# Decode attention over a cached 268 MB of keys and values: units of eight heads with 64 KB value runs, in place of units of four heads with 32 KB tiles

## The chip, the cores and the metric

The kernel runs on one core of one Trainium2 chip. The metric is the device time of one execution in microseconds (us), the median over runs. Every time below comes from those runs, from the profile of one execution, or from that execution's trace.

## What is computed

Four sequences (B = 4) of one token each, model width D = 640, 32 query heads and 32 key/value heads of 128, a cache of 4096 positions, all in bfloat16. The input is normalized, and attention and a small gated MLP both start from it:

```python
xn = _layernorm(x)
# A: attention with a cache
q = (xn @ wq).reshape(B, 1, 32, 128)                     # per head
scores = einsum('bhqd,bhkd->bhqk', q, k_cache) * 128 ** -0.5
p = softmax(scores)                                      # over 4096 positions
attn = einsum('bhqk,bhkd->bhqd', p, v_cache).reshape(B, 1, 4096) @ wo
# B: gated MLP (spatial size 1)
z = gelu(xn @ w_in); z1, z2 = z[..., :864], layernorm(z[..., 864:])
mlp = (z1 * (w_sp * z2 + b_sp)) @ w_out
out = x + attn + mlp
```

The two caches hold 4 x 32 x 4096 x 128 x 2 bytes each, 134 MB. Each byte of them is needed once.

## The kernel before

**Units.** A unit is one sequence and four neighbouring heads (HT = 4), and there are NT = 32 of them, sequence fastest: unit i has sequence i % 4 and head group i // 4. The four heads' keys, 16384 rows of 128 numbers, lie in one stretch of HBM. They are cut over the 128 partitions so that partition p holds rows 128 p to 128 p + 127: 32 partitions ("lanes") for each head, one contiguous run of 32 KB for each partition. Values are laid out in the same way. A key tile or a value tile is thus 128 x 32 KB, 4 MB, one DMA on the SP queue.

**Places.** One pool of `KV_SLOTS = 5` places of 32 KB per partition serves keys and values in turn (`load`, L115); at the start three of the places hold the query weight (in two DMAs) and the MLP's weights. `pump` (L137) issues the next loads of a written list for as long as the occupant of the place, five loads earlier, has been used. The list is k0, k1, v0, k2, v1, k3 and so on, with two extra keys near the end (`EXTRA_K`), so that the last loads are values. The SP queue takes its instructions in the order written, each waiting for the readers of its place. Eight semaphores go round among the DMAs, so that a DMA also waits until the one eight before it has landed. The last value tile is loaded in four pieces (`V_CUTS`), and behind it the output weight of the last head group in four (`load_wo`, L147); the other groups' output weights are loaded one group at a time.

**One iteration (L568).** The order on PE, DVE, ACT and SP is written out by hand. For key tile i, each half of 64 rows per partition in turn:
- `product` (L399): DVE multiplies the half in place by the query, which `stage_q` (L379) has spread over the lanes two units earlier (one matmul that copies a row of queries to all partitions, then four ACT copies, one for each head's lanes).
- `fold_half` (L409): DVE adds the upper 64 numbers of each row to the lower.
- `sums` (L418): eight PE matmuls with the identity add up 64 columns to 8 in PSUM.
- `row_sums` (L429): DVE adds those 8 to the score.

Then `head_max` (L436) finds each head's maximum by a reduction, a transpose among 32 partitions and another reduction, and `exps` (L445) makes the exponentials, one ACT instruction for each head with its sum. They are written into `p_m`, a matrix of 32 columns for each group of four row positions (two sequences x four positions x four heads, zero where a head doesn't live on the partition), with which `weighted` (L462) multiplies a value tile: 32 matmul groups of 128 x 512. `weighted` for tile i runs in the iteration after its keys (later near the end). `take`, `group_den`, `group_pick`, `group_turn` and `group_proj` bring a finished head group of four sequences into the right shape, divide it by the sums and multiply it by the output weight into one PSUM tile that lives through the whole kernel.

**The ends.** Before the loop stand the normalization, the query projection (`q_rows`) and `gmlp`. After the loop, the last value tile is used position by position (`o_last`, L625) as its pieces land, then the last group's projection (L530), two copies and two output DMAs follow.

Of the kernel before, what the change touches and what calls it, by code (L numbers as in the profile page):

```python
# [12 lines left out]
ALU = mybir.AluOpType  # L13
AX = mybir.AxisListType

KV_SLOTS = 5
EXTRA_K = (24, 28)
WO_BUFS = 2
# [3 lines left out]
def kernel(  # L22
# [26 lines left out]
    HT = 4  # L49
    HG = H // HT  # L50
    NT = HG * Bsz
    LN = P // HT
    NC = HT * S // P
    HC = NC // 2
    HD2 = Dh // 2
# [6 lines left out]
    QD = 32  # L62
    CB = 4
    NG = NC // CB
    GW = CB * Dh
    MC = CB * HT

    const = ctx.enter_context(tc.tile_pool(name="const", bufs=1))
    kv = ctx.enter_context(tc.tile_pool(name="kv", bufs=KV_SLOTS))
    wop = ctx.enter_context(tc.tile_pool(name="wop", bufs=WO_BUFS))  # L70
# [5 lines left out]
    ps_m = ctx.enter_context(tc.tile_pool(name="ps_m", bufs=3, space=PSUM))  # L76
    ps_out = ctx.enter_context(tc.tile_pool(name="ps_out", bufs=1, space=PSUM))

    def slot(name):
        return kv.tile([P, SLOT], BF16, tag="kv", name=name)  # L80
# [4 lines left out]
    wq_v = A_wq.rearrange("(p c) n -> p c n", c=DC)  # L85
    wq_parts = []
    for c0, c1 in ((0, HT), (HT, DC)):
        t = slot("wq")[:, 0 : (c1 - c0) * HD].rearrange("p (c n) -> p c n", n=HD)
        nc.sync.dma_start(out=t, in_=wq_v[:, c0:c1, :])
        wq_parts += [(t, i) for i in range(c1 - c0)]  # L90
# [6 lines left out]
    w_sb = slot("w_sb")  # L97
    w_in_sb = w_sb[:, 0 : DC * F].rearrange("p (c n) -> p c n", c=DC)
    w_out_sb = w_sb[:, DC * F : DC * F + NFC * D].rearrange("p (k n) -> p k n", k=NFC)
# [6 lines left out]
    def kv_view(cache, i):  # L106
        hg, b = divmod(i, Bsz)
        return cache[b, HT * hg : HT * (hg + 1)].rearrange("h s d -> (h s) d").rearrange(
            "(p c) d -> p (c d)", c=NC
        )  # L110
# [4 lines left out]
    def load(which, i):  # L115
        cache, tiles = (A_k_cache, k_tiles) if which == "k" else (A_v_cache, v_tiles)
        t = slot("k_nat" if which == "k" else "v_nat")
        cuts = V_CUTS if (which, i) == ("v", NT - 1) else (0, NC)
        for c0, c1 in zip(cuts, cuts[1:]):
            nc.sync.dma_start(  # L120
                out=t[:, c0 * Dh : c1 * Dh], in_=kv_view(cache, i)[:, c0 * Dh : c1 * Dh]
            )
        tiles[i] = t[:].rearrange("p (c d) -> p c d", d=Dh)

    loads = [("k", 0), ("k", 1)]
    n_k = 2
    for i in range(NT):
        loads.append(("v", i))
        for _ in range(2 if i + 1 in EXTRA_K else 1):
            if n_k < NT:  # L130
                loads.append(("k", n_k))
                n_k += 1
    occupants = [("w", 0), ("w", 1), ("w", 2)] + loads
    used = set()
    n_loaded = [0]

    def pump():  # L137
        while n_loaded[0] < len(loads):
            at = n_loaded[0] + 3 - KV_SLOTS
            if at >= 0 and occupants[at] not in used:  # L140
                return
            load(*loads[n_loaded[0]])
            n_loaded[0] += 1
# [3 lines left out]
    def load_wo(j):  # L147
        wo_tiles[j] = wop.tile([P, HT, D], BF16, name="wo")
        rows = A_wo[j * HT * P : (j + 1) * HT * P]
        if j == HG - 1:  # L150
            by_head = rows.rearrange("(h p) n -> p h n", p=P)
            for hh in range(HT):
                nc.sync.dma_start(out=wo_tiles[j][:, hh, :], in_=by_head[:, hh, :])
            return
        nc.sync.dma_start(out=wo_tiles[j][:], in_=rows.rearrange("(p j) n -> p j n", j=HT))
# [5 lines left out]
    ones_row = const.tile([1, P], FP32)  # L161
    nc.vector.memset(ones_row[:], 1.0)
# [6 lines left out]
    p_m = [const.tile([P, NG, QD], BF16, name=f"pm{b}") for b in range(Bsz)]  # L169
    acc = [const.tile([P, HT, QD], FP32, name=f"acc{g}") for g in range(NACC)]  # L170
    for t in acc:
        nc.gpsimd.memset(t[:], 1.0)
        nc.gpsimd.memset(t[:, :, 0:Bsz], 0.0)
# [35 lines left out]
    QB = HG // CB  # L209
    q_rows = []  # L210
    for r in range(QB):
        q_ps = ps_pv.tile([P, GW], FP32, tag="pv", name="q_ps")
        for c in range(DC):
            t, i = wq_parts[c]
            for g in range(CB):
                hg = r * CB + g
                nc.tensor.matmul(  # L217
                    out=q_ps[g * QD : (g + 1) * QD, :],
                    lhsT=xnT[:, c, :],
                    rhs=t[:, i, hg * GW : (hg + 1) * GW],  # L220
                    start=(c == 0),
                    stop=(c == DC - 1),
                )
        rows = const.tile([P, GW], BF16, name=f"q_rows{r}")
        nc.vector.tensor_copy(out=rows[:], in_=q_ps[:])  # L225
        q_rows.append(rows)

    pick = const.tile([P, 2, CB, HT, QD], FP32)
    nc.vector.memset(pick[:], 0.0)
    hot = work.tile([P, 2, MC], FP32, name="hot")  # L230
    nc.vector.tensor_reduce(
        out=hot[:],
        in_=ident[:].rearrange("p (g t m) -> p t m g", g=P // QD, t=2),
# [3 lines left out]
    for a in range(2):  # L237
        for t in range(2):
            nc.vector.tensor_copy(
                out=pick[:, a, :, :, 2 * a + t],  # L240
                in_=hot[:, t, :].rearrange("p (c h) -> p c h", c=CB),
            )
# [17 lines left out]
    for name in ("zz", "gw", "gt", "gz"):  # L260
        gm[name] = work.tile([P, 2, NFC, Bsz], FP32, name=name)
    nc.gpsimd.memset(gm["zz"][:], 0.0)
    gm["sq"] = work.tile([P, NFC, Bsz], FP32, name="sq")
# [4 lines left out]
    def gmlp():  # L268
        zz, gw, gt, gz, sq = (gm[n] for n in ("zz", "gw", "gt", "gz", "sq"))
# [26 lines left out]
        nc.vector.tensor_tensor(out=gz[:], in0=zz[:], in1=gt[:], op=ALU.mult)  # L296
        nc.vector.tensor_tensor(out=sq[:], in0=gz[:, 1, :, :], in1=gz[:, 1, :, :], op=ALU.mult)

        s_ps = ps_m.tile([1, 2 * Bsz], FP32, tag="m", name="ln_ps")
        for src, at in ((gz[:, 1, :, :], 0), (sq[:], Bsz)):  # L300
            for k in range(NFC):
                nc.tensor.matmul(
                    out=s_ps[:, at : at + Bsz],
                    lhsT=ones_sq[:, 0:1],
                    rhs=src[:, k, :],
                    start=(k == 0),
                    stop=(k == NFC - 1),
                )
# [5 lines left out]
        tmp_t = st[:, 4 * Bsz : 5 * Bsz]  # L314
        nc.vector.tensor_scalar(
            out=st[:, 0 : 2 * Bsz],
            in0=s_ps[:],
# [28 lines left out]
            out=ac_ps[:], lhsT=ones_row[:], rhs=ac[:], start=True, stop=True  # L346
# [4 lines left out]
            out=sq[:],  # L351
# [5 lines left out]
            out=sq[:],  # L357
            in0=sq[:],
# [3 lines left out]
        nc.vector.tensor_tensor(out=gm["yT"][:], in0=gz[:, 0, :, :], in1=sq[:], op=ALU.mult)  # L362
# [11 lines left out]


# [3 lines left out]
    def stage_q(i):  # L379
        hg, b = divmod(i, Bsz)  # L380
        r, g = divmod(hg, CB)
        row = g * QD + b
        qb_ps = ps_m.tile([P, HT, Dh], FP32, tag="m", name="qbc_ps")
        nc.tensor.matmul(  # L384
            out=qb_ps[:],
            lhsT=ident[:, row : row + 1].to_broadcast([P, P]),
            rhs=q_rows[r][:],
            start=True,
            stop=True,
        )  # L390
        qbcs[i] = small.tile([P, Dh], BF16, name="qbc", bufs=3)
        for hh in range(HT):
            ps = slice(hh * LN, (hh + 1) * LN)
            nc.scalar.copy(out=qbcs[i][ps, :], in_=qb_ps[ps, hh, :])  # L394
# [4 lines left out]
    def product(i, half):  # L399
# [3 lines left out]
            in1=qbcs[i][:, None, :].to_broadcast([P, HC, Dh]),  # L403
# [22 lines left out]
    def row_sums(i, half):  # L426
        if half == 0:
            scores[i] = small.tile([P, NC], FP32, name="s_sb")
        nc.vector.tensor_reduce(  # L429
            out=scores[i][:, half * HC : (half + 1) * HC],  # L430
            in_=sums_ps.pop((i, half))[:],
            axis=AX.X,
            op=ALU.add,
        )

    def head_max(i):  # L436
        m1 = small.tile([P, 1], FP32, name="m1")
        nc.vector.tensor_reduce(out=m1[:], in_=scores[i][:], axis=AX.X, op=ALU.max)  # L438
        mt = small.tile([P, LN], FP32, name="mt")
        nc.vector.transpose(out=mt[:], in_=m1[:].to_broadcast([P, LN]))  # L440
        nm = small.tile([P, 1], FP32, name="nm")
        nc.vector.tensor_reduce(out=nm[:], in_=mt[:], axis=AX.X, op=ALU.max, negate=True)  # L442
        maxes[i] = nm

    def exps(i):  # L445
        hg, b = divmod(i, Bsz)
        nb = small.tile([P, 1], FP32, name="nb")
        nc.scalar.mul(out=nb[:], in_=maxes.pop(i)[:], mul=scale_qk)  # L448
        s_sb, a = scores.pop(i), acc[hg % NACC]
        pm = p_m[b][:].rearrange("p g (t c h) -> p g t c h", t=2, c=CB)  # L450
        for hh in range(HT):
            ps = slice(hh * LN, (hh + 1) * LN)
            nc.scalar.activation(  # L453
                out=pm[ps, :, b % 2, :, hh],
                in_=s_sb[ps, :].rearrange("p (g c) -> p g c", c=CB),
                func=ACT.Exp,
                bias=nb[ps],
# [216 lines left out]
```

## Time and profile before

| | |
|---|---|
| time, median of 3 runs | 666.97 us (666.65 to 667.26) |
| the profiled execution | 666.78 us, its span 665.0 us |
| read from HBM | 282.24 MB, 424 GB/s over the span |
| SP queue's packets | 11928, 99.2% of 16 engines' span |
| busy: PE, DVE, ACT | 309.9, 499.5, 127.1 us |
| chain that ended last | DMA 68%, DVE 23%, PE 6% |
| first packet starts, last ends | 1.76 us, 661.35 us |

The packet records give the size and the time of every packet. One contiguous run of a partition is one packet:

| bytes | packets on SP's queue | median ns |
|---|---|---|
| 4 (end of a DMA) | 1332 | 9 |
| 1280 | 608 | 55 (mean 57.5) |
| 4096 | 256 | 162 |
| 5120 | 896 | 200 (mean 199) |
| 8192 | 256 | 309 |
| 16384 | 128 | 614 |
| 17280 | 128 | 644 |
| 32768 | 8192 | 1216 (mean 1221) |

How to read the profile's lines: in the slices, a line has 40 values for 40 equal parts of the span. In a table of stretches, a row has the stretch, its length, the busy time of PE, PEld (weight load), DVE, ACT and POOL with the number of instructions, the granted TensorE clock, the mean busy share of the 16 DMA engines and what they moved. In a timeline, a row has start and duration in us, engine, line and operation, and what is written from what; SPq is the SP queue's issue of a DMA. A bracket gives the idle time before and what ended it.

### The profile page before, as it was taken

Reading aid. Unit: us, or ns where it says so; the run is one execution under the profiler, and the core shown is the slowest. Engines: PE = TensorE matmul, PEld = TensorE weight load, DVE = VectorE, ACT = ScalarE, POOL = GpSimd, SP = SyncE. Lnnn points to the kernel's source line nnn. Section 1 sums busy time; section 2 is a strip of 40 time slices with the busy share of each in tenths; the row PEclk is TensorE's granted clock in tenths of the full one; section 3 lists DMA queues with packets and bytes.
Section 4 is the critical chain, followed back from the end, with each engine's and each line's share of the span. In section 5 each row is a group of like instructions: output and inputs, shape, how many; then the busy total and the mean of one; then the engine's idle time right before and its main releaser. Section 6 shows DMA issues by size and latency. Waiting matters only on the chain.

```text
span 665.0 us, 5142 instructions
## 1 busy us (share of the span) xinstructions
PE 309.9 (47%) x2033; PEld 130.3 (20%) x2033; DVE 499.5 (75%) x350; ACT 127.1 (19%) x441; POOL 4.7 (1%) x15
## 2 busy tenths in 40 slices
PE   2536443445436235553238443355443655338466
PEld 1312111211112111321113111131111312113124
DVE  2299797877788777788777697777787899776970
ACT  0302222102222111222111222111222122111121
POOL 2000000000000000000000000000000000000000
PEclk9656766877767777776776856788765678776575
DMA  9999999999999999999999999999999999999996
GB/s 367 430 440 417 434 436 426 433 430 429 436 420 440 426 430 437 426 431 428 432 433 424 435 434 424 438 421 440 427 430 436 423 436 426 433 432 430 431 430 274
DMA packets 11972, 282.58 MB, mean 425 GB/s; under 512 B 1344, under 2 KB 1964, under 8 KB 3244
## 3 DMA queue, kind: packets, MB, share of 16 engines
q1 hardware_dynamic: 11928, 282.25, 99.2%
q8 instruction: 16, 0.26, 0.2%
q14 instruction: 8, 0.07, 0.0%
q10 hardware_dynamic: 20, 0.01, 0.0%
HBM read 282.24 MB, written 0.01 MB: 424 GB/s over the span
## 4 chain that ended last, share of the span: by engine, by line
DMA 68%; DVE 23%; PE 6%; issue 2%; SPq 0%; DVEq 0%
DMA k_nat<-in_A_k_cache_dram 62%; DVE k_nat L400 12%; DVE k_nat L409 7%; PE s_ps L418 4%; DMA v_nat<-in_A_v_cache_dram 4%; DVE s_sb L429 2%; DMA wq<-in_A_wq_dram 2%; PE pv L470 1%; PE q_ps L217 1%; DVE m L438 0%; DVE mt L440 0%; DVE o_n L513 0%; DVE nm L442 0%; PE out_ps L530 0%; SPq L120 0%
## 5 line engine op out<-in xcount | busy, mean ns | idle before, releaser
L400 DVE TENSOR_TENSOR k_nat<-k_nat,qbc 128x8192 bf16<-128x8192 bf16 x64 | 282.7, 4417 | 104.6 <-DMA k_nat<-in_A_k_cache_dram 104.3
L418 PE MATMUL s_ps<-k_nat,ident 128*128 128x512 bf16 x512 | 183.8, 523 | 327.0 <-DVE k_nat L409 327.0
L418 PEld LDWEIGHTS <-ident 128*128 128x128 bf16 x512 | 62.3, 122 | 430.7 <-issue 356.8
L409 DVE TENSOR_TENSOR k_nat<-k_nat 128x4096 bf16<-128x4096 bf16 x64 | 146.0, 2281 | 0.0
L448 ACT ACTIVATE nb<-nm 128x1 f32<-128x1 f32 x32 | 6.5, 203 | 355.1 <-DVE nm L442 355.1
L470 PE MATMUL pv<-v_nat,pm 128*32 128x512 bf16 x992 | 71.0, 438 | 3.7 <-DMA v_nat<-in_A_v_cache_dram 3.7
L453 ACT ACTIVATE pm<-s_sb,nb 32x128 bf16<-32x128 f32 x128 | 71.7, 560 | 2.7
L394 ACT CAST qbc<-qbc_ps 32x128 bf16<-32x128 f32 x128 | 32.8, 256 | 133.1 <-PE qbc_ps L384 132.0
L429 DVE TENSOR_REDUCE s_sb<-s_ps 128x64 f32<-128x512 f32 x64 | 43.6, 682 | 3.1 <-PE s_ps L418 3.1
L470 PEld LDWEIGHTS <-pm 128*32 128x32 bf16 x992 | 25.9, 109 | 55.3 <-issue 36.9
L453 ACT ACTIVATION_READ_ACCUMULATOR pm<-s_sb,nb 32x1 f32 x128 | 30.1, 235 | 0.0
L502 PEld LDWEIGHTS o_ps<-o_rows,pick 128*128 128x128 f32 x112 | 20.1, 269 | 2.1 <-issue 1.4
L502 PE MATMUL o_ps<-o_rows,pick 128*128 128x128 f32 x112 | 19.5, 347 | 0.0
L384 PE MATMUL qbc_ps<-q_rows,ident 128*128 128x512 bf16 x32 | 17.5, 552 | 0.0
L482 ACT COPY o_rows<-pv 128x512 f32<-128x512 f32 x16 | 9.4, 585 | 27.5 <-PE pv L470 27.5
L494 DVE RECIPROCAL rden<-den 128x1 f32<-128x1 f32 x7 | 1.2, 168 | 15.6 <-PE den L486 15.6
L438 DVE TENSOR_REDUCE m<-s_sb 128x1 f32<-128x128 f32 x32 | 9.2, 286 | 1.1
L225 DVE CAST q_rows<-q_ps 128x512 bf16<-128x512 f32 x2 | 1.4, 692 | 10.6 <-PE q_ps L217 10.6
L440 DVE STREAM_TRANSPOSE mt<-m 128x32 f32<-128x32 f32 x32 | 6.8, 212 | 1.1
L217 PE MATMUL q_ps<-wq,xnT 128*32 128x512 bf16 x40 | 4.1, 552 | 7.3 <-DMA wq<-in_A_wq_dram 7.3
L442 DVE TENSOR_REDUCE nm<-mt 128x1 f32<-128x32 f32 x32 | 6.0, 186 | 1.1
L384 PEld LDWEIGHTS <-ident 128*128 128x128 bf16 x32 | 4.4, 141 | 8.6 <-issue 8.6
(83 smaller groups left out, 73.4 us busy)
## 6 DMA issues: line engine op xcount, KB each, us to landing
k_nat<-in_A_k_cache_dram SPq DMA_DIRECT2D x32, 4096.0 KB, 41.2
v_nat<-in_A_v_cache_dram SPq DMA_DIRECT2D x31, 4096.0 KB, 35.7
wo<-in_A_wo_dram SPq DMA_DIRECT2D x7, 640.0 KB, 42.3
wq<-in_A_wq_dram SPq DMA_DIRECT2D x1, 4096.0 KB, 12.8
w_sb<-in_B_w_in_dram SPq DMA_DIRECT2D x1, 2160.0 KB, 19.5
v_nat<-in_A_v_cache_dram SPq DMA_DIRECT2D x1, 2048.0 KB
wq<-in_A_wq_dram SPq DMA_DIRECT2D x1, 1024.0 KB, 14.8
v_nat<-in_A_v_cache_dram SPq DMA_DIRECT2D x1, 1024.0 KB
```

The costliest lines, as they stand in the source:

```text
L217: nc.tensor.matmul(out=q_ps[g * QD : (g + 1) * QD, :], lhsT=xnT[:, c, :], rhs=t[:, i, hg * GW : (hg + 1) * GW], start=(c == 0), stop=(c == ...
L384: nc.tensor.matmul(out=qb_ps[:], lhsT=ident[:, row : row + 1].to_broadcast([P, P]), rhs=q_rows[r][:], start=True, stop=True,)
L394: nc.scalar.copy(out=qbcs[i][ps, :], in_=qb_ps[ps, hh, :])
L400: nc.vector.tensor_tensor(out=half_of(i, half), in0=half_of(i, half), in1=qbcs[i][:, None, :].to_broadcast([P, HC, Dh]), op=ALU.mult,)
L409: nc.vector.tensor_tensor(out=t[:, :, 0:HD2], in0=t[:, :, 0:HD2], in1=t[:, :, HD2:Dh], op=ALU.add)
L418: nc.tensor.matmul(out=s[:], lhsT=ident[:], rhs=t[:, :, g * RW : (g + 1) * RW], start=(g == 0), stop=(g == n - 1),)
L429: nc.vector.tensor_reduce(out=scores[i][:, half * HC : (half + 1) * HC], in_=sums_ps.pop((i, half))[:], axis=AX.X, op=ALU.add,)
L438: nc.vector.tensor_reduce(out=m1[:], in_=scores[i][:], axis=AX.X, op=ALU.max)
L453: nc.scalar.activation(out=pm[ps, :, b % 2, :, hh], in_=s_sb[ps, :].rearrange("p (g c) -> p g c", c=CB), func=ACT.Exp, bias=nb[ps], scale= ...
L470: nc.tensor.matmul(out=pvs[hg, a][cg * QD : (cg + 1) * QD, :], lhsT=pm[:, g, :], rhs=v_nat[:, g * CB : (g + 1) * CB, :], start=(t == 0 and ...
L482: nc.scalar.copy(out=o[:].rearrange("p c d -> p (c d)"), in_=pvs.pop((hg, a))[:])
L502: nc.tensor.matmul(out=o_ps[:], lhsT=pick[:, a, c, :, :].rearrange("p h q -> p (h q)"), rhs=o[:, c, :], start=(a == 0 and c == 0), stop=(a ...
```

## The change

A unit is now one sequence and eight heads (HT = 8, NU = 16 units), 16 lanes for each head, and a partition's contiguous run is 64 KB, 256 rows. Every group of 32 partitions holds two heads.

- Values: a unit's 64 KB run per partition is one DMA into the only place of the pool `vp`. Keys: a run is still loaded as two tiles of 32 KB per partition (tile 2u and 2u + 1, each half of every partition's run), into three places of the pool `kp`. The last unit's values come as two halves into key places.
- Loads: k0, k1, k2, then for each unit its values and two keys, three at unit `AHEAD` = 8. `pump` waits for the holder of the place in the ring that the load belongs to.
- The query weight and w_in lie in the value place at the start, the query weight as one DMA of 40 KB per partition; w_out lies in the only place of the output weight, which is now loaded for eight heads at a time, the last group row by row in five DMAs.
- `stage_q` selects the right head's query for each lane by a mask matrix in two accumulated matmuls, and one ACT copy follows. The queries carry the factor 128 ** -0.5 already.
- `head_max`, `exps` work on a unit (two key tiles) at a time. In a group of 32 partitions, each of the two heads has an exponential of its own over all 32 partitions, and a bias of about -1e30 on the other head's 16 lanes makes those zero.
- `weighted` runs over a unit's 64 matmul groups, two iterations after the unit's first key tile up to unit 8, three after it from unit 9; `pick_unit` gathers each unit's rows, and a group (now four units of eight heads) is turned and projected in the iteration after its last unit.
- In `gmlp`, the 14 small matmuls with a column of ones become one, followed by a reduction on DVE.

The diff, cut to its core:

```diff
-KV_SLOTS = 5
-EXTRA_K = (24, 28)
-WO_BUFS = 2
+K_SLOTS = 3
+AHEAD = 8
...
-    HT = 4
+    HT = 8
+    PAR = HT // NQ
+    LN = P // HT
     HG = H // HT
-    NT = HG * Bsz
-    LN = P // HT
-    NC = HT * S // P
+    NU = HG * Bsz
+    NR = HT * S // P
+    NC = NR // 2
     HC = NC // 2
+    NT = 2 * NU
...
+    kp = ctx.enter_context(tc.tile_pool(name="kp", bufs=K_SLOTS))
+    vp = ctx.enter_context(tc.tile_pool(name="vp", bufs=1))
+    wop = ctx.enter_context(tc.tile_pool(name="wop", bufs=1))
...
+    w_a = vp.tile([P, 2 * SLOT], BF16, tag="v", name="w_a")
+    wq_sb = w_a[:, 0 : DC * HD].rearrange("p (c n) -> p c n", c=DC)
+    w_in_sb = w_a[:, DC * HD : DC * (HD + F)].rearrange("p (c n) -> p c n", c=DC)
+    w_b = wop.tile([P, HT, D], BF16, tag="wo", name="w_b")
+    w_out_sb = w_b[:, 0:NFC, :]
+    nc.sync.dma_start(out=wq_sb, in_=A_wq.rearrange("(p c) n -> p c n", c=DC))
...
+    def load(which, n):
+        if which == "k":
+            k_tiles[n] = half_run(kp.tile([P, SLOT], BF16, tag="k", name="k_nat"), A_k_cache, n)
+        elif which == "v":
+            t = vp.tile([P, 2 * SLOT], BF16, tag="v", name="v_nat")
+            nc.sync.dma_start(out=t[:], in_=run_of(A_v_cache, n))
+            v_tiles[n] = t[:].rearrange("p (c d) -> p c d", d=Dh)
+        else:
+            t = kp.tile([P, SLOT], BF16, tag="k", name="v_end")
+            cuts = V_CUTS if n % 2 else (0, NC)
+            v_tiles["h", n] = half_run(t, A_v_cache, n, cuts)
+
+    loads = [("k", 0), ("k", 1), ("k", 2)]
+    n_k = 3
+    for u in range(NU - 1):
+        loads.append(("v", u))
+        for _ in range(3 if u == AHEAD else 2):
             if n_k < NT:
                 loads.append(("k", n_k))
                 n_k += 1
+    loads += [("h", NT - 2), ("h", NT - 1)]
     used = set()
     n_loaded = [0]
+    holders = {"k": [], "v": [("w", 0)]}
 
     def pump():
         while n_loaded[0] < len(loads):
+            which, n = loads[n_loaded[0]]
+            ring, slots = (holders["v"], 1) if which == "v" else (holders["k"], K_SLOTS)
+            if len(ring) >= slots and ring[-slots] not in used:
                 return
+            load(which, n)
+            ring.append((which, n))
             n_loaded[0] += 1
...
+            for h0, h1 in ((0, 4), (4, 5), (5, 6), (6, 7), (7, 8)):
+                nc.sync.dma_start(out=wo_tiles[hg][:, h0:h1, :], in_=by_head[:, h0:h1, :])
             return
+        nc.sync.dma_start(
+            out=wo_tiles[hg][:].rearrange("p (e j) n -> p e j n", e=PAR),
+            in_=rows.rearrange("(e p j) n -> p e j n", e=PAR, j=JR),
+        )
...
+    def exps(u):
+        hg, b = divmod(u, Bsz)
+        s_sb, a, nb = scores.pop(u), acc[hg % NACC], maxes.pop(u)
+        for k in range(NQ):
+            ps = slice(k * QD, (k + 1) * QD)
+            for e in range(PAR):
+                h = PAR * k + e
+                at = Bsz * (h // NQ) + b
+                nc.scalar.activation(
+                    out=p_m[u % 2][ps, :, :, h],
+                    in_=s_sb[ps, :].rearrange("p (g c) -> p g c", c=CB),
+                    func=ACT.Exp,
+                    bias=nb[ps, e : e + 1],
+                    scale=1.0,
+                    accum_out=a[ps, h % NQ, at : at + 1],
+                )
...
     turns = {}
+    for u in range(NU - 1):
+        turns[2 * u + (3 if u > AHEAD else 2)] = u
...
+            if due is not None:
+                if due % Bsz == Bsz - 1:
+                    group_den(due // Bsz)
+                weighted(due, v_tiles[due], range(NG))
+                take(due)
+                used.add(("v", due))
             used.add(("k", i))
             pump()
-            if i % Bsz == 2 and i // Bsz < HG - 1:
-                load_wo(i // Bsz)
+            if i % (2 * Bsz) == 4 and i // (2 * Bsz) < HG - 1:
+                load_wo(i // (2 * Bsz))
         load_wo(HG - 1)
```

## The prediction

> **What bounds the kernel now.** I read the page first: the busy row of the engines, the slices, the DMA lines and the chain.
>
> ```profile
> span 665.0 us, 5142 instructions
> ...
> PE 309.9 (47%) x2033; PEld 130.3 (20%) x2033; DVE 499.5 (75%) x350; ACT 127.1 (19%) x441; POOL 4.7 (1%) x15
> ...
> GB/s 367 430 440 417 434 436 426 433 430 429 436 420 440 426 430 437 426 431 428 432 433 424 435 434 424 438 421 440 427 430 436 423 436 426 433 432 430 431 430 274
> DMA packets 11972, 282.58 MB, mean 425 GB/s; under 512 B 1344, under 2 KB 1964, under 8 KB 3244
> ```
>
> No engine is near full (DVE 75%), and between the first and the last slice the transfer rate stands still around 430 GB/s. Is the DMA ever idle in there? The busy times by stretches answer it; the last two columns are DMA share and GB/s.
>
> ```profile
> 20.00:80.00 60.00, 28.86 (x225) 13.41 (x226) 47.24 (x43) 13.29 (x38) 0.00 (x0) 0.60 1.01 431
> 80.00:320.00 240.00, 106.28 (x672) 42.67 (x669) 183.91 (x117) 45.19 (x162) 0.00 (x0) 0.74 1.00 431
> 320.00:560.00 240.00, 110.92 (x634) 45.39 (x635) 191.45 (x123) 46.57 (x169) 0.00 (x0) 0.71 1.00 430
> 560.00:650.00 90.00, 47.43 (x277) 19.24 (x276) 69.92 (x47) 17.63 (x62) 0.00 (x0) 0.69 1.00 429
> ```
>
> Share 1.00 throughout: the 16 DMA engines have work at every moment. The packet records say the same from the other end: packets run from 1.76 to 661.35 us, 659.6 us, with all 16 engines occupied save at the two ends. So the time is 1.76 us until the first packet, 659.6 us of packets, 3.7 us after the last, and 1.78 us outside the span (666.78 for this execution; the median of the three is 0.19 above that). Compute work that the change saves is worth nothing unless it lies in the 3.7 us; what counts is (a) engine time per packet, (b) whether the queue runs dry, (c) the tail.
>
> **(a) Packets.** Medians of the packet records: 8192 B 309 ns, 16384 B 614, 32768 B 1216. Twice 614 less 1216 is 12 ns that a longer packet saves; per byte it is (1216-614)/16384 = 0.0367 ns, so 32 KB are 1204 ns of bytes and 12 of fixed cost. On one engine each packet starts 3 to 4 ns before the one before it ends, which leaves 8.5 ns; and 28% of the 32 KB packets take about 8 ns more (1224), about one in four whatever the data, worth 2 ns per packet. I take 10.5 ns per packet saved.
>
> Each transfer of 128 partitions gives each engine 8 packets. Fifteen value units become one 64 KB run per partition where there were two tiles of 32 KB: 15 x 8 = 120 packets fewer per engine, -1.26 us. No packet over 32 KB is in the trace, so the bounds are: all 12 ns plus 2 saved, -1.7 us; or every 64 KB packet like two of the slow ones, 2 x (1224-1218.6) = +10.8 ns, +1.3 us. I take the row's law, since three doublings obey it. The Trainium skill (DMA: Bandwidth & Descriptors, "Why small descriptors are slow") gives the fixed part as about three bus cycles and 32 bytes of metadata; as an estimate at this trace's 1.18 ns per 32 bytes that is 4.7 ns, and the sum below would come to 666.4.
>
> The smaller items, by the same net times: the query weight as one 40 KB run instead of 32 + 8, 8 packets fewer, -0.08. Output weight: before 56 packets of 5 KB (199 ns) and 32 of 1280 B (57.5); after 48 and 64, since the last group, loaded row by row, is now eight heads: 48 x 195.5 + 64 x 54 less 56 x 195.5 + 32 x 54 = +0.16. Transfers on the queue fall from 83 to 64, each with one 4-byte packet of 9 ns (5.5 net): -0.10. The keys keep 32 KB packets, at twice the pitch in HBM: 0, as the last value tile does it now: its first cut reads 16 KB at a 32 KB pitch at 614 ns, half of a full one and the fixed 12. Sum of (a): -1.28 us.
>
> **(b) Does the one value place starve the queue?** Now a place is free some 40 ns after its last reader, and a transfer takes 36 to 41 us from issue to landing, four deep:
>
> ```profile
> 77.43 0.33 SPq L120 DMA_DIRECT2D v_nat<-in_A_v_cache_dram  x1
> 81.14 0.33 SPq L120 DMA_DIRECT2D k_nat<-in_A_k_cache_dram  x1
> 81.51 0.43 SPq L155 DMA_DIRECT2D wo<-in_A_wo_dram  x1
> 97.39 0.33 SPq L120 DMA_DIRECT2D v_nat<-in_A_v_cache_dram  x1
> ```
>
> After: value unit u+1 can be issued only when `weighted(u)` is done, and behind it on SP stand the key tiles that follow, which DVE waits for. A key tile takes 8 x 1.221 = 9.8 us, a value unit 19.5. An iteration takes DVE 15.4 us (48.60 to 64.02), its last sums 1.7 more. Let key tile 2u+2 land at 0. Its predecessor landed at -9.8, so the iteration runs from 5.6 to 21 and its sums end at 23; value unit u has landed at 19.5. `weighted(u)` is 64 matmul groups: two units of 32 back to back took 4.86 us, so 28. Its eight exponentials have from 12 to 23 us; one with its read took 0.58 us for 128 columns, at twice the columns at most 1.16 each, 9.3. At 28 the queue still holds two key tiles, to 39. From issue to first packet is 1.0 us (0.74 to 1.76): 10 us of cover in every unit. Past unit 8 the same order holds, one iteration later.
>
> The first unit is tightest. Keys 0 and 1 land at 34.8 and 44.5 as now, key 2 at 54.3, value 0 (its place free at 25.0, when the gMLP's first matmuls end) at 73.8, keys 3 and 4, issued at 52.3 and 65.7 as the first two iterations end, at 83.6 and 93.4. Iteration 2 ends as now at 79.2, its sums at 81.1, `weighted(0)` at about 85.5: 7 us to spare with the issue. The query rows wait for the whole weight (16.0 instead of 13.6 us) and end at 20.1; w_in lands at 21.2, so that is hidden by 1.1 us, and beyond it by value 0's margin. The end: value unit 14 is issued at 28 of its cycle like the others, the two halves of the last unit go to key places freed in iterations 29 and 30, 10 us and more ahead of need. So (b) is 0.
>
> **(c) Tail.** Now the last value piece lands at 660.09 and the last output-weight piece at 661.84, 0.5 us after the last packet; the last matmul waits for that:
>
> ```profile
> 660.77 0.17 DVE L633 TENSOR_TENSOR o_n_last<-o_last,rden_all 128x16 bf16<-128x16 f32 x1 [6.17 <-PE o_last L625]
> ...
> 661.00 1.32 PE L530 MATMUL out_ps<-wo,o_n_last 128*4 128x320 bf16 x8 [0.27 <-DVE o_n_last L633]
> 661.89 0.08 PEld L530 LDWEIGHTS <-o_n_last 128*4 128x4 bf16 x1 [0.27 <-issue]
> ```
>
> After, 64 x 57.5 ns = 3.7 us of output weight follow the last value piece, so that lands 3.1 us before the last packet's end. Then 0.9 us to the projection and 16 matmuls of 0.165 (1.32/8): 0.45 us past the last packet, when its last piece is just landing (0.5). Both ways the PE ends about 1.0 us past the last packet: 0.
>
> The sum: span 665.0 - 1.28 = 663.7; + 1.78 outside = 665.5; + 0.19 to the median = **665.7**, 0.19% less. A measurement of this kernel tells about 0.2% (1.3 us) from no change, so the forecast lies on that border. The exponentials, head maxima and copies that the change halves or merges lie beside the DMA and bring nothing.
>
> **Rivals.** *No longer packets.* If a 64 KB run crosses as two of 32 KB, only the small items are left, -0.02: 666.9. For it: no packet above 32 KB in the trace. Against: 17280 B runs go as one. 14%.
>
> *Key pitch.* Each key tile now reads 32 KB out of every 64 KB; were the 16 engines' streams, which run in step, to meet in the same part of HBM, the 32 key tiles (313 us) would slow. At the lowest inner slice, 417 of 430 GB/s, that is 3%, +9.4: 675. The Trainium skill's page DMA: Bandwidth & Descriptors ("Latency and other measured facts") speaks for it: it lists lower rates at large power-of-two pitches, beginning with 207 of 214 GB/s at 512 KiB, far above ours. Against: the 614 ns above. 8%.
>
> *The queue runs dry (slower).* Should the value place be handed over later than I reckon, say one iteration, 15.4 us: if only in the first unit, 15.4-7 = +8.4, 674; if in all, 15.4-10 = 5.4 x 14, 741. It decides from 10 us of lateness on (7 in the first unit). Against: every term of (b) has a row. 9%.
>
> **Chances.** Forecast case 62%, with its own range 665.0 to 666.4, half of it beyond the border; 7% for what I have not seen (how evenly 16 engines end: they lose 1.2 us on average now). Faster 0.39, same 0.40, slower 0.21. The range goes down to 664.6 (the bound of -1.7 and a luckier end) and up to 668.2 (the bound of +1.3 on the second case); the two slow rivals stay outside.
>
> **What would show it.** Right: about 1,900 packets fewer for the values (some 10,000 in all), packets of 65536 B at 2420 to 2430 ns, DMA share 1.00 from 20 to 650 us, wo's landing still ahead of the last matmul. Wrong: a packet count near 11,900 (first rival); 32 KB packets over 1216 in the keys (second); a share under 1.00 between two value units, with SP waiting on PE pv (third).

## The result, and the profile after

The changed kernel took 674.35 us (median of 4 runs, 672.0 to 676.48) against 666.98 before: a ratio of 1.011, 95% interval 1.0064 to 1.0155. It is 1.1% slower, where 665.7, 0.2% faster, was forecast. The profiled execution took 672.0 us with a span of 670.2. One execution of all below, of key_earlier (688.85 us), fell in a slower state of the chip and is left out of that run's median and ratio.

The page of the changed kernel first, the lines that were shown of before:

```profile
span 670.2 us, 4854 instructions
...
PE 332.3 (50%) x1999; PEld 132.9 (20%) x1999; DVE 489.4 (73%) x305; ACT 184.9 (28%) x297; POOL 6.3 (1%) x16
...
GB/s 374 426 430 464 407 463 413 453 403 439 438 424 448 414 456 419 434 450 397 464 420 433 431 424 446 428 435 444 419 451 415 440 437 417 452 421 449 417 410 60
DMA packets 10002, 282.56 MB, mean 422 GB/s; under 512 B 1040, under 2 KB 2172, under 8 KB 3324
...
DMA 50%; DVE 35%; PE 11%; ACT 2%; issue 1%; SPq 1%; DVEq 0%; ACTq 0%
```

There are 10002 packets, so the values do cross as 64 KB runs (1920 packets of 65536 B, median 2418 ns). In the slices the last one has 60 GB/s where it had 274, and ACT, which lost a third of its instructions, is busier: 184.9 us against 127.1. The busy times by stretches (last two columns DMA share and GB/s) say where the DMA stops:

```profile
80.00:320.00 240.00, 125.00 (x731) 48.34 (x730) 180.49 (x100) 68.64 (x112) 0.00 (x0) 0.67 1.00 432
320.00:560.00 240.00, 117.23 (x608) 45.10 (x608) 192.44 (x108) 66.31 (x107) 0.00 (x0) 0.66 1.00 433
560.00:650.00 90.00, 46.95 (x290) 17.83 (x289) 60.99 (x38) 28.42 (x45) 0.00 (x0) 0.63 1.00 431
650.00:657.00 7.00, 2.45 (x22) 1.27 (x26) 0.36 (x1) 4.47 (x8) 0.00 (x0) 0.50 0.87 335
657.00:670.00 13.00, 9.31 (x172) 6.40 (x160) 0.68 (x2) 1.00 (x2) 0.00 (x0) 0.50 0.02 5
```

The share is 1.00 up to 650 us: the one value place starves nothing. The last large packet ends at 657.86 us, 3.5 us earlier than before (661.35). But the kernel then goes on for 12.3 us, where it had 3.7: +8.7. Both together are the 5.2 us between the spans. This is the end of it, in the timeline of the changed kernel:

```profile
639.87 0.69 DVE L467 TENSOR_REDUCE s_sb<-s_ps 128x64 f32<-128x512 f32 x1 [3.66 <-PE s_ps L454]
...
643.57 0.59 ACT L517 COPY o_rows<-pv 128x512 f32<-128x512 f32 x1 [20.49 <-PE pv L505]
644.18 1.43 ACT L492 ACTIVATE pm<-s_sb,nb 32x256 bf16<-32x256 f32 x1
...
652.90 1.59 ACT L492 ACTIVATE pm<-s_sb,nb 32x256 bf16<-32x256 f32 x1
654.02 0.48 ACT L492 ACTIVATION_READ_ACCUMULATOR pm<-s_sb,nb 32x1 f32 x1
654.55 0.64 PE L646 MATMUL den_all<-acc,ones_sq 128*128 128x32 f32 x2 [9.29 <-ACT pm L492]
655.12 3.60 PE L505 MATMUL pv<-v_end,pm 128*32 128x512 bf16 x32
658.83 0.59 ACT L517 COPY o_rows<-pv 128x512 f32<-128x512 f32 x1 [4.34 <-PE pv L505]
659.47 1.87 PE L582 MATMUL o_last<-hot,o_rows 128*128 128x8 f32 x8 [0.75 <-ACT o_rows L517]
661.20 3.56 PE L660 MATMUL o_last<-pm,v_end 128*128 128x8 bf16 x128
664.80 0.19 DVE L668 TENSOR_TENSOR o_n_last<-o_last,rden_all 128x32 bf16<-128x32 f32 x1 [9.21 <-PE o_last L660]
665.04 2.30 PE L566 MATMUL out_ps<-wo,o_n_last 128*4 128x320 bf16 x16 [0.28 <-DVE o_n_last L668]
```

The last eight exponentials run from 644.18 to 654.5. Before, the last four ran from 647.4 to 649.7, and when the last value piece landed at 660.09, 16 small matmuls were left:

```profile
649.17 0.56 ACT L453 ACTIVATE pm<-s_sb,nb 32x128 bf16<-32x128 f32 x1
649.50 0.23 ACT L453 ACTIVATION_READ_ACCUMULATOR pm<-s_sb,nb 32x1 f32 x1
...
660.14 0.59 PE L625 MATMUL o_last<-pm,v_nat 128*128 128x4 bf16 x16 [0.67 <-DMA v_nat<-in_A_v_cache_dram]
```

Here, after the change, at 654.5, when the last value piece has just landed, all of unit 15's values are still to be multiplied. Nothing waits for a DMA any more; each line waits for the line above it. The groups by form show what made the exponentials long, before and after, with the mean ns of one in front of the second bar:

```profile
L453 ACT ACTIVATE pm<-s_sb,nb 32x128 bf16<-32x128 f32 x128 | 71.7, 560 | 2.7
```

```profile
L492 ACT ACTIVATE pm<-s_sb,nb 32x256 bf16<-32x256 f32 x128 | 164.6, 1520 | 226.6 <-DVE nb L481 225.2
```

As many instructions, twice the columns, 2.7 times the time. With its accumulator read, which partly overlaps, one took 0.58 us and takes 1.30.

### The profile page after: what moved, and what is told of

It reads as the page before. It is cut to its first block, busy times and chain, and to the rows that moved or that the text cites. A ratio compares the mean times of both kernels' runs of the same rounds, so it can differ in the third digit from the quotient of the medians.

```text
span 670.2 us, 4854 instructions
## 1 busy us (share of the span) xinstructions
PE 332.3 (50%) x1999; PEld 132.9 (20%) x1999; DVE 489.4 (73%) x305; ACT 184.9 (28%) x297; POOL 6.3 (1%) x16
## 2 busy tenths in 40 slices
DMA packets 10002, 282.56 MB, mean 422 GB/s; under 512 B 1040, under 2 KB 2172, under 8 KB 3324
## 4 chain that ended last, share of the span: by engine, by line
DMA 50%; DVE 35%; PE 11%; ACT 2%; issue 1%; SPq 1%; DVEq 0%; ACTq 0%
DMA k_nat<-in_A_k_cache_dram 50%; DVE k_nat L436 21%; DVE k_nat L445 10%; PE pv L505 5%; PE s_ps L454 5%; DVE s_sb L467 3%; ACT pm L492 2%; PE o_last L660 1%; DVE m L473 0%; PE out_ps L566 0%; SPq L131 0%; PE o_last L582 0%; DVE mt L475 0%; DVE nm L479 0%; ACT o_rows L517 0%
## 5 line engine op out<-in xcount | busy, mean ns | idle before, releaser
L454 PE MATMUL s_ps<-k_nat,ident 128*128 128x512 bf16 x512 | 221.9, 611 | 292.1 <-DVE k_nat L445 292.1
L492 ACT ACTIVATE pm<-s_sb,nb 32x256 bf16<-32x256 f32 x128 | 164.6, 1520 | 226.6 <-DVE nb L481 225.2
L492 ACT ACTIVATION_READ_ACCUMULATOR pm<-s_sb,nb 32x1 f32 x128 | 62.6, 489 | 0.0
L505 PE MATMUL pv<-v_nat,pm 128*32 128x512 bf16 x960 | 61.1, 412 | 0.0
L536 PE MATMUL o_ps<-o_rows,pick 128*128 128x128 f32 x96 | 13.9, 288 | 8.9 <-ACT o_rows L517 8.9
L536 PEld LDWEIGHTS o_ps<-o_rows,pick 128*128 128x128 f32 x96 | 11.6, 191 | 14.8 <-ACT o_rows L517 14.8
L473 DVE TENSOR_REDUCE m<-s_sb 128x1 f32<-128x256 f32 x16 | 6.7, 420 | 0.6
L582 PE MATMUL o_last<-hot,o_rows 128*128 128x8 f32 x32 | 5.0, 285 | 3.0 <-ACT o_rows L517 3.0
L422 PE MATMUL qbc_ps<-q_rows,of_row 128*128 128x128 bf16 x32 | 6.2, 284 | 0.6 <-DVE q_rows L250 0.6
L566 PE MATMUL out_ps<-wo,o_t 128*4 128x320 bf16 x48 | 6.2, 431 | 0.0
```

Of the source, the lines that this page charges most:

```text
L422: nc.tensor.matmul(out=qb_ps[:], lhsT=of_row[:, e, b].rearrange("p k f l -> p (k f l)"), rhs=q_rows[e][:, hg, :], start=(e == 0), stop=(e ...
L454: nc.tensor.matmul(out=s[:], lhsT=ident[:], rhs=t[:, :, g * RW : (g + 1) * RW], start=(g == 0), stop=(g == n - 1),)
L473: nc.vector.tensor_reduce(out=m1[:], in_=scores[u][:], axis=AX.X, op=ALU.max)
L492: nc.scalar.activation(out=p_m[u % 2][ps, :, :, h], in_=s_sb[ps, :].rearrange("p (g c) -> p g c", c=CB), func=ACT.Exp, bias=nb[ps, e : e + 1],
L505: nc.tensor.matmul(out=pvs[u][cg * QD : (cg + 1) * QD, :], lhsT=p_m[u % 2][:, g].rearrange("p c h -> p (c h)"), rhs=v_at[:, n * CB : (n + ...
L536: nc.tensor.matmul(out=gr[hg][:], lhsT=pick[:, c, Bsz - 1 - b : P + Bsz - 1 - b], rhs=o[:, c, :], start=(b == 0 and c == 0), stop=(b == Bs ...
```

## The experiments

The theory after the result, "tail": past the last key tile the chain of compute (head maximum, exponentials, two halves of values, projection) is longer than the DMA that covers it, mostly by the exponentials. The rivals: the hand-over of the one value place, and the clock granted to PE, 0.68 instead of 0.72.

**Order on ACT alone (take_later).**

```diff
-                take(due)
+                if i < NT - 1:
+                    take(due)
...
         exps(NU - 1)
+        take(NU - 2)
         picked(NU - 2)
```

> The changed kernel, with the copy of value unit 14's result (take, on ACT) moved behind the last unit's exponentials. Theory 'tail': the end is set by the chain from the last key tile (DVE, head maximum, eight exponentials, last two value halves, projection), not by the DMA; in it the exponentials stood ready from 641.7 us and began at 644.2, behind the copy that waits for unit 14's matmuls. Then the time falls by 2.5 us. Rival 'value place': the loss lies in the hand-over of the one value place between units; then no change. Rival 'clock': the PE was granted less (0.68 instead of 0.72); then no change.

671.34 us (7 runs, 670.11 to 677.08), ratio 1.0085 (1.0057 to 1.0114). The exponentials began at 641.57, 2.6 us earlier, and the median is 3.0 us lower, but the span of the profiled execution fell only from 670.2 to 669.0, and the interval overlaps that of the changed kernel. In the order written for PE, unit 14's gathering, now waiting for the late copy, stood ahead of unit 15's values, which began at 654.87 instead of 655.12:

```profile
651.96 0.59 ACT L517 COPY o_rows<-pv 128x512 f32<-128x512 f32 x1
652.60 1.88 PE L582 MATMUL o_last<-hot,o_rows 128*128 128x8 f32 x8 [8.19 <-ACT o_rows L517]
```

The step in the chain is real; most of the gain was given back at the next one. By itself this run is inconclusive.

**An earlier key tile (key_earlier).**

```diff
+AHEAD2 = 12
-        for _ in range(3 if u == AHEAD else 2):
+        for _ in range(3 if u in (AHEAD, AHEAD2) else 2):
-        turns[2 * u + (3 if u > AHEAD else 2)] = u
+        turns[min(2 * u + 2 + (u > AHEAD) + (u > AHEAD2), NT - 1)] = u
```

> The changed kernel with a second extra key ahead (three keys after value unit 12 too), so that the last key tile but one is loaded before value unit 13. Theory 'tail': DVE, which waited 9 us for that tile, starts on it when it is free (597.5 instead of 606.5 us) and on the last one when it lands (616), not at 621.9: the chain is 5 to 6 us shorter, the time about 5 us less. Rival 'value place': value unit 13 is read and its place freed later, so no gain or slower by up to 10 us. Rival 'clock': no change.

676.25 us (3 runs, 674.88 to 681.14), ratio 1.0159 (1.0115 to 1.0203): no gain over the changed kernel, whose interval it overlaps. That is a miss for "tail", and what "value place" had said. DVE did start at 596.84 instead of 606.46, and the stretch after the last packet shrank from 12.3 to 9.2 us. But the packets ended 7.4 us later, at 665.30: value unit 13 was read an iteration later, and unit 14, the next in the queue, could be issued only at 619.5, when the queue had been empty since 615:

```profile
605.00:615.00 10.00, 6.21 (x15) 2.06 (x15) 7.31 (x4) 8.37 (x14) 0.00 (x0) 0.67 0.82 355
615.00:620.00 5.00, 4.45 (x66) 1.60 (x64) 4.32 (x1) 0.50 (x1) 0.00 (x0) 0.89 0.00 0
```

So the hand-over of one place does cost when its cover is used up. In the changed kernel it isn't.

**Short exponentials (exp_run4).** The columns of `p_m` in another order, and the selecting matrix with them:

```diff
-    p_m = [const.tile([P, NG, CB, HT], BF16, name=f"pm{n}") for n in range(2)]
+    p_m = [const.tile([P, NG, HT, CB], BF16, name=f"pm{n}") for n in range(2)]
...
-                    out=p_m[u % 2][ps, :, :, h],
+                    out=p_m[u % 2][ps, :, h, :],
```

> The changed kernel with the columns of p_m in the order head, position instead of position, head, so that an exponential writes runs of four neighbours (8 bytes) instead of single 2-byte numbers 16 bytes apart; the selecting matrices follow. An exponential with its read takes 1.30 us after the change (256 columns) and took 0.58 before (128 columns, 8 bytes apart): more than double. Theory 'tail' with 'write stride': one falls to 0.8 or less, eight of them to 6.4 us from 10.4, and the time falls by 4 us or more. If the length comes from the columns alone or from the masked lanes, one stays at 1.30 and the time stays.

666.34 us (10 runs, 664.4 to 673.42), ratio 0.9997 (0.9974 to 1.0021), 8.0 us below the changed kernel's median; the profiled span fell by 5.6 us, to 664.6. The same instruction on the same 256 columns, with the same masks:

```profile
L492 ACT ACTIVATE pm<-s_sb,nb 32x256 bf16<-32x256 f32 x128 | 63.6, 497 | 226.9 <-DVE nb L481 225.6
```

497 ns instead of 1520, and 0.56 us from one to the next. So it is neither the number of columns nor the masked lanes: it is where the 2-byte results go. 16 bytes apart they cost 1.30 us for 256, in runs of four 0.56.

**The same in the kernel before (before_run4).** `(t c h)` becomes `(t h c)` in its `p_m`.

> The kernel before with its p_m columns in the order sequence, head, position, so that an exponential writes runs of four neighbours instead of single numbers 8 bytes apart. Write stride theory: an exponential of 128 columns falls from 0.58 us with its read to 0.4 or less. The time stays at 666.9 within 0.2%, since the DMA sets it and the four exponentials end 10 us ahead of the last value piece.

One exponential takes 398 ns instead of 560 (0.50 us with its read, not the 0.4 expected), and the time is 666.94, ratio 1.0 (0.9991 to 1.0009). The layout was costly before as well, but the DMA covered it.

**Both orders at the end (tail_order).** exp_run4, ACT as in take_later, and on PE unit 14's gathering behind the first half of unit 15's values:

```diff
         weighted(u, v_tiles["h", NT - 2], range(NG // 2))
+        picked(NU - 2)
         take(u)
```

> The changed kernel with exponentials that write runs of four (as in exp_run4), and with the end put in another order: on ACT unit 14's copy behind the last exponentials, on PE unit 14's gathering behind the first half of unit 15's values. Theory 'tail': the exponentials start at 641.3 instead of 644.5 us and end near 645.5, the values' first half runs from about 646 to 650, the last half then keeps up with its landing pieces (the last at 654.8), the projection ends near 660: the DMA (last packet at 657.7) sets the end again, the span is 661 to 662, the time 663 to 664, 0.5% below before, and the times scatter as little as those of before. Rival 'value place' or 'clock': no gain over exp_run4 (666.3).

663.17 us (5 runs, 663.10 to 663.22), ratio 0.9943 (0.993 to 0.9956): 0.6% faster than the kernel before, and its runs lie within 0.12 us where those of the changed kernel spread over 4.5. The exponentials end at 645.7, and the projection waits for a transfer again:

```profile
655.04 0.19 DVE L670 TENSOR_TENSOR o_n_last<-o_last,rden_all 128x32 bf16<-128x32 f32 x1 [8.46 <-PE o_last L662]
656.10 2.30 PE L566 MATMUL out_ps<-wo,o_n_last 128*4 128x320 bf16 x16 [1.10 <-DMA wo<-in_A_wo_dram]
```

The value place is as it was, and the granted clock 0.69 where the changed kernel had 0.68 (exp_run4, granted 0.66, was shorter than the changed kernel too): as causes of the loss both rivals fall.

**What the long run is worth (tail_order_v32).**

```diff
-            nc.sync.dma_start(out=t[:], in_=run_of(A_v_cache, n))
+            for c0 in (0, SLOT):
+                nc.sync.dma_start(out=t[:, c0 : c0 + SLOT], in_=run_of(A_v_cache, n)[:, c0 : c0 + SLOT])
```

> tail_order with each value unit loaded by two DMAs of 32 KB per partition into the same place, nothing else changed: packets of 32 KB instead of 64. By the prediction's law (10.5 ns for each of 120 packets, and 15 more end packets of 5.5 ns) it is 1.3 us slower than tail_order. If 64 KB packets save nothing beside the 8 ns that the records show (2 x 1213 - 2418), 0.5 to 1 us. If the 32 KB packets fall back to 1216 and 1224, as before the change, 120 x (2 x 1218.6 - 2418) = 2.3 us, and then it is the long run that takes the slow ones away.

663.99 us (12 runs, 663.75 to 664.86 and one of 668.29): the 64 KB run is worth 0.8 us here, by the medians; the slowest of tail_order's five runs is 0.5 us below the fastest of these. The 32 KB packets stay at 1213. The change's DMA had gained 3.5, so something else gave the larger part.

**Where the other 2.7 us came from (before_again, before_pitch, before_align, tail_order_32off).**

> The kernel before once more, for its packet records. After the change a 32 KB packet takes 1213 ns where it took 1216, with one in four at 1224, and the packets end at 657.9 us instead of 661.4: 3.5 us less, where I had worked out 1.3. If the loads' layout does it, 32 KB packets are at 1216 and 1224 again here. If it is a matter of the execution or the chip, they are at 1213 here too and the packets end near 659.

The kernel before showed 1216 and 1224 ns again, last packet at 661.39: it belongs to the program.

> The kernel before, with key and value tile i read as halves of every partition's 64 KB run (32 KB out of every 64 KB, as the changed kernel reads keys) instead of one closed stretch; rows thus come to lanes of other heads, and the output is not the reference's. Same instructions, same packets of 32 KB. Theory 'pitch helps': the 1216 and 1224 ns of the kernel before come from the closed stretch; then all packets take 1213 here and the time falls by 8192 x (1221.4-1214)/16 = 3.8 us, to 663. Rival: it is something else in the change (64 KB packets between, fewer DMAs, other places); then 1216 and 1224 stay and the time with them.

666.85 us, ratio 0.9999 (0.999 to 1.0008), packets at 1216 and 1224: not the pitch. Of what is left, where the packets go in their partitions was tried next, in the kernel before:

```diff
+    pad = const.tile([P, 56], FP32)
+    nc.gpsimd.memset(pad[:], 0.0)
     eps_tile = const.tile([P, 1], FP32)
```

> The kernel before with an unused tile of 224 bytes per partition ahead of the others, so that all places of keys, values and output weight begin at a multiple of 256 bytes in their partition; in the kernel before they begin 32 bytes past one, in the changed kernel on one. Theory 'alignment': the 1216 and 1224 ns come from those 32 bytes; then 32 KB packets take 1213, and the time falls by 8192 x (1221.4-1214)/16 = 3.8 us less what the last pieces' own chain holds back, to 663 to 664.5. Rival: something else in the change (fewer DMAs, other places); then 1216 and 1224 and the time of 666.8 stay.

663.48 us, ratio 0.995 (0.9936 to 0.9964), the 32 KB packets at 1213. An unused tile of 224 bytes makes the kernel before 0.5% faster. The other way round, with an unused tile of 32 bytes in tail_order:

> tail_order with an unused tile of 32 bytes per partition ahead, so that its places begin 32 bytes past a multiple of 256, as in the kernel before. Theory 'alignment': 32 KB packets go from 1213 to 1216 and 1224, the 64 KB packets by at least as much, and the DMA ends 2.5 us later: 665.5 instead of 663.2. Rival: no change.

666.1 us, ratio 0.9989 (0.998 to 0.9998): 2.9 us slower than tail_order, 32 KB packets at 1216 and 1224, those of 64 KB at 2421 and up to 2428. So the larger part of what the change's DMA gained came from tiles that it happened to move by 32 bytes, not from long runs.

## Why the prediction was wrong, step by step

**(c), the tail, at 0: this step failed.** It started from the last value piece and asked only what follows its landing, taking for granted that the exponentials of the last unit were done by then. Their own chain, from the last key tile through the head maximum, was not followed. It could have been, from the terms of (b): eight exponentials at the bound of 1.16 us are 9.3 us against 2.3 before, and behind them the values' first half, which before had been worked on tile by tile, then the whole of the second half and twice the projection. Measured, the stretch after the last large packet is 12.3 us instead of 3.7. Where that chain is out of the way, (c)'s own sum comes out: in tail_order the projection ends at 658.40, 1.0 us past the last packet (657.40). The closing sentence of the sum, that the exponentials "lie beside the DMA and bring nothing", is true of 15 units and false of the last, whose chain runs on past the last packet.

**The exponential, "at most 1.16": mis-sized.** Twice the columns was taken as at most twice the time; it was 1.30 us, 2.2 times. This alone is the smaller part: at 1.16 the eight would have ended 1.1 us earlier, of the 8.7 lost at the end (an estimate, 8 x 0.14). The spacing of the results in `p_m`, doubled from 8 to 16 bytes, was in the diff and was not priced. With runs of four, exp_run4 took 5.6 us off the span; the two orders of tail_order, which let PE and ACT go on without waiting for unit 14, another 3.3 (664.6 to 661.3).

**(a), packets: right sign, both terms off.** Forecast -1.28 us, measured -3.5. The long runs, put at -1.26, were worth 0.8 (tail_order against tail_order_v32). By the records a 64 KB packet saves 8 ns (2 x 1213 - 2418) where the prediction had 12. Less the 3 to 4 ns by which one packet starts before the other's end, that is 4 to 5 ns, 0.5 to 0.6 us over 120 packets (an estimate), where the prediction took 10.5: the row's 2 ns for the slow packets was not theirs to save. Nor do the three doublings of the row all obey one law: 2 x 309 - 614 is 4 ns, not 12. The 0.82 us in time are 6 to 7 ns per packet; where the rest comes from isn't shown. The Trainium skill's price (DMA: Bandwidth & Descriptors, "Why small descriptors are slow"), 4.7 ns as the estimate there, agrees with the 4 to 5 ns of the records.

Missing altogether was the start of the places, 32 bytes past a multiple of 256 before and on one after: 2.7 us by difference, 2.9 and 3.4 in the two runs made for it. The 28% of slow packets, "about one in four whatever the data", were its mark, taken as given. tail_order_32off is the kernel without either surprise, its end in order and its places 32 bytes off: 666.1 us, 0.4 from the forecast.

**(b), the queue: right.** `weighted(0)` was forecast to end at about 85.5; the next value load was issued at 86.43. The DMA share is 1.00 up to 650. key_earlier shows that the margin was of the size reckoned: one iteration more, and the queue is dry for 5.2 us (615.3 to 620.5), where one iteration less the cover, 15.4 - 10, is 5.4.

**The rivals.** Key pitch: fell (before_pitch, and the keys' packets at 1213); the falling rates at large pitches that the Trainium skill lists (DMA: Bandwidth & Descriptors, "Latency and other measured facts") begin at 512 KiB. At 64 KB nothing of the kind is seen here: 666.85 us with it, 666.83 without. No longer packets: fell, 2418 ns for 65536 B. The queue running dry: fell, the share is 1.00 up to 650. That the 674.35 measured is the figure of the two slow rivals (675 and 674) is chance; the slowdown came at a place that no rival named.

**Open.** The changed kernel's four runs fall in two pairs, at 672.0 and 672.3 and at 676.4 and 676.5 us, and why is not shown. The long pair was granted less of the clock (0.66 against 0.67 to 0.68), but in exp_run4 the longest run, 673.42 us, had 0.670, more than each of its six runs of 666.1 to 666.9. tail_order's five runs and tail_order_32off's eleven show one level; one of tail_order_v32's twelve, with the same end, does not (668.29 us). tail_order also ran on another chip than exp_run4, though the kernel before took the same time on both (666.83 and 666.86). That the second level comes from the compute at the end, where PE is granted 0.50, is a guess.

## What to carry to other kernels

In this kernel, which the DMA fills, compute counted at the end: follow the chain from the last input of every stream, not only from the last to land. When units are made larger, the chain of the last one grows with them; making that one small would be a way out, not tried here. A layout of results that looks free in the middle can be paid there. Before a few tenths of a per cent are put down to an edit, compare the packets' own times: a tile that moves by 32 bytes can be worth more than the edit.

## What the runs showed of the hardware

- ACT writing 2-byte results: 128 of them 8 bytes apart took 560 ns, 256 of them 16 bytes apart 1520, in runs of four (8 bytes) 398 and 497. The columns and the masks are the same in 1520 and 497 (exp_run4 changes the layout alone); a law for other spacings was not measured.
- A DMA's target that begins 32 bytes past a multiple of 256 in its partition: 32 KB packets 1216 ns, one in four 1224, against 1213; 1280 B 57.5 against 55; 2.9 and 3.4 us in all. Which multiple is needed was not separated: a place 32 bytes past a multiple of 256 is also 32 past one of 64. The weights' packets in the first 20 us don't show it (17280 B 644 ns either way); why not is open.
